# 64 unused bytes per partition between the weight buffers and the buffers of split tokens

## The chip, the cores and the metric

The kernel runs on one core of a Trainium2 chip. The metric is the device time of one execution in microseconds; the time before is the median of three runs. One more execution was taken with the hardware profiler, and all rows below come from it.

## What is computed

The reference is attention with a sigmoid in place of the softmax, for 8 batches of 12 heads with 448 tokens and 64 features a head, followed by a layer that takes the maximum of three products and multiplies it by an output matrix:

```python
scores = q @ k.T / sqrt(64) - log(448)
x = (1 / (1 + exp(-scores))) @ v          # then heads side by side: 3584 x 768
h = maximum(maximum(x @ w1, x @ w2), x @ w3)
out = h @ w_out                           # all four matrices 768 x 768
```

Everything is float32.

## The kernel before

**Two stages.** Attention runs first, 24 steps of four heads each; the results go to DRAM. Behind it runs the maxout stage: four matrices (w1, w2, w3 and the output matrix), each multiplied with the tokens of eight batches. The stage is tiled in visits: 4 groups of output columns (`STAGES`) times 4 pairs of batches, 16 visits; in each visit three products `q`, and each of these by a scheme of Strassen's kind, with seven block products (`PRODUCTS`) instead of eight. The operands of the block products are sums and differences of blocks: `a11`, `s2`, ... for weights, `b11`, `t2`, ... for tokens.

**Split operands.** Each operand is kept as two float32r tiles, a rounded `hi` and the remainder `lo`; a block product is the sum of lo x hi, hi x lo and hi x hi over three blocks of 128 features, which makes 9 matmuls of 128 x 128 weights by 448 token columns. So the stage has 16 x 3 x 7 x 9 = 3024 matmuls, all issued by one line, 476, in `product`. Weights are the stationary operand, tokens the moving one. Two of the 3024 are made 30 columns wider (`wide`, 478 columns): the first matmul of block product 1 in visit 0, and the first of block product 4 in visit 11, second product. The 30 extra columns are read from the next block of the same tile, and their results are used by nobody.

**What is where in SBUF.** Pools take their place in the order in which they are opened. These stay for the whole kernel: `w` (42 tiles of split weights, 7 operands x 3 products x hi and lo, 1536 bytes per partition each), `ws` (weights before the split, 1536 bytes each), `xs` (tokens before the split, 5376 bytes each), `m` (4 result tiles of 1792 bytes), and `xo` (hi and lo of the first two token operands, 5376 bytes each). Behind `xo` come attention's pools, which are closed at its end: `qk`, `hl`, `dec`, `sq`, `v`, `a`. Their place is taken by the maxout stage's further pools: `xs2`, `xo2` (hi and lo of the other five token operands), `c` and `dec2`. A matmul of line 476 reads 128 columns of weights at `k * P` (512 bytes times k) and a block of tokens at `xt[:, k]` (1792 bytes times k).

**Order.** Every instruction is pinned to program order on its engine, so the order of work is the order of the text. All loads and stores but half of the last one are issued by SyncE; VectorE computes the `lo` tiles (lines 121, 231, 294), ScalarE the sigmoid (282), the `hi` tiles (227) and copies out of PSUM (583), GpSimd the sums of blocks (108, 196).

In attention, line 312 computes the scores as three float32r products, in pairs of two matmuls with 64 rows of weights each; lines 336 and 347 weigh the values in plain float32. All operands of these lines come from pools that are opened behind `xo`.

Of the kernel before, what the change touches and what calls it, by code (L numbers as in the profile page):

```python
# [8 lines left out]
F32 = mybir.dt.float32  # L9
# [8 lines left out]
P = 128  # L18
D = 64

LEAST = 1.125 * 2.0**-15

PRODUCTS = (
    ("a11", "b11", 0),
# [10 lines left out]
def attention_then_maxout(  # L35
# [30 lines left out]
    def pool(stack, name, bufs, **kw):  # L66
        return stack.enter_context(tc.tile_pool(name=name, bufs=bufs, **kw))
# [2 lines left out]
    ws_p = pool(ctx, "ws", 1)  # L70
    xs_p = [pool(ctx, "xs", 1)]
    m_p = pool(ctx, "m", 1)
    xo_p = [pool(ctx, "xo", 1)]
    ps_av = pool(ctx, "ps_av", 1, space=PSUM)

# [47 lines left out]
    def decoding(dec_p, todo, bufs, ahead, square_p):  # L123
# [11 lines left out]
        def decode(raw, out):  # L135
# [17 lines left out]
            pin(nc.vector.scalar_tensor_tensor(  # L153
                out=out, in0=square, scalar=LEAST**2, in1=bits.bitcast(F32),
                op0=ALU.is_ge, op1=ALU.mult,
# [504 lines left out]
```

## Time and profile before

| | |
|---|---|
| median of three runs | 864.51 us (864.01 to 864.61) |
| profiled execution, span from first to last instruction | 861.9 us |
| TensorE matmul busy | 857.6 us, 99% |
| VectorE, ScalarE, GpSimd busy | 619.9, 413.3, 173.5 us |
| maxout stage (line 476) in the chain that ended last | 613.13 us of it |

The profiled span leaves out what lies before the first and behind the last instruction; it stands 2.6 us under the median. "PE" is TensorE's matmuls and "PEld" its weight loads, which run beside them; a matmul's own duration in the trace is longer than the distance to the next one, since matmuls are pipelined, so pace is read from the starts. The names of tiles are cut at their first digit or so: `xhi_t` stands for all `hi` tiles of the token operands t1 to t4, `whi_s` for the weights s1 to s4. `a<-b` is written from b.

### The profile page before, as it was taken

The page shows a single profiled execution, that of the slowest core. Times are in us where ns is not written, and L with a number is a line of the kernel's source. Part 1 is how long each engine was busy: PE and PEld are TensorE (multiplying, and loading weights), DVE is VectorE, ACT ScalarE, POOL GpSimd, SP SyncE. Part 2 cuts the span into 40 slices and gives each one's busy share as a digit, 9 for nine tenths or more (in the row PEclk, how much of TensorE's full clock was granted, in tenths as well). Part 3 has the DMA queues.
Part 4 walks back from the last instruction along what each step waited for, and adds up shares of the span by engine and source line. Part 5 has one row for each costly group of instructions (what it writes and reads, how often), then busy time and mean ns, then how long its engine had stood idle before and what let it go on. Part 6 is the DMA issues. An engine that isn't in the chain of part 4 may idle for free.

```text
span 861.9 us, 14260 instructions
## 1 busy us (share of the span) xinstructions
PE 857.6 (99%) x5446; PEld 706.5 (82%) x5446; DVE 619.9 (72%) x885; ACT 413.3 (48%) x545; POOL 173.5 (20%) x148
## 2 busy tenths in 40 slices
PE   9999999999999999999999999999999999999998
PEld 5555555555579999999999999999999999999997
DVE  5677668877795775787887698778778887736542
ACT  6888888888862340423434252234325252423310
POOL 0010020202115337121000021200002544560600
PEclk9999999999999999999999999999999999999999
DMA  8657776786684537326563823465472516153412
GB/s 293 209 209 242 246 253 231 257 295 220 214 288 175 184 147 250 125 75 205 207 248 113 324 80 97 161 254 198 161 290 99 186 43 238 69 202 123 154 65 86
DMA packets 74628, 161.96 MB, mean 188 GB/s; under 512 B 6976, under 2 KB 54080, under 8 KB 74560
## 3 DMA queue, kind: packets, MB, share of 16 engines
q1 hardware_dynamic: 74416, 160.94, 53.0%
q8 instruction: 43, 0.70, 0.3%
q14 instruction: 25, 0.20, 0.1%
q10 hardware_dynamic: 144, 0.11, 0.0%
HBM read 109.90 MB, written 51.12 MB: 187 GB/s over the span
## 4 chain that ended last, share of the span: by engine, by line
PE 99%; DVE 0%; DVEq 0%; issue 0%
PE ps_y L476 71%; PE ps_s L312 9%; PE ps_s L336 7%; PE ps_av L336 6%; PE ps_s L347 2%; PE ps_s L325 2%; PE ps_av L312 2%; PE ps_s L383 0%; PE ps_av L325 0%; PE ps_av L347 0%; DVE m L548 0%; DVEq L656 0%
## 5 line engine op out<-in xcount | busy, mean ns | idle before, releaser
L476 PE MATMUL ps_y<-xhi_t,whi_s 128*128 128x448 f32 x432 | 157.9, 365 | 0.0
L476 PE MATMUL ps_y<-xhi_t,wlo_s 128*128 128x448 f32 (+1 forms) x432 | 157.8, 365 | 0.0
L476 PE MATMUL ps_y<-xlo_t,whi_s 128*128 128x448 f32 x432 | 157.8, 365 | 0.0
L282 ACT ACTIVATE a<-ps_s,bias_s 128x896 f32<-128x896 f32 x121 | 114.5, 1016 | 10.2 <-PE ps_s L312 10.2
L476 PE MATMUL ps_y<-xhi_b,wlo_a 128*128 128x448 f32 x288 | 105.3, 366 | 0.0
L476 PE MATMUL ps_y<-xlo_b,whi_a 128*128 128x448 f32 x288 | 105.2, 365 | 0.0
L476 PE MATMUL ps_y<-xhi_b,whi_a 128*128 128x448 f32 x288 | 105.2, 365 | 0.0
L583 ACT COPY p<-ps_y 128x448 f32<-128x448 f32 x48 | 25.5, 531 | 157.6 <-PE ps_y L476 157.6
L108 POOL TENSOR_TENSOR ws_s<-ws_a,ws_a 128x384 f32<-128x384 f32 x12 | 14.2, 1180 | 417.9 <-DMA ws_a<-w_dram 312.8
L476 PEld LDWEIGHTS ps_y<-xhi_t,whi_s 128*128 128x128 f32 x432 | 81.2, 188 | 6.4
L476 PEld LDWEIGHTS ps_y<-xlo_t,whi_s 128*128 128x128 f32 x432 | 81.2, 188 | 6.4
L476 PEld LDWEIGHTS ps_y<-xhi_t,wlo_s 128*128 128x128 f32 x432 | 81.2, 188 | 6.3
L557 DVE TENSOR_TENSOR m<-ps_y,u 128x448 f32<-128x448 f32 x71 | 43.9, 621 | 53.3 <-PE ps_y L476 53.3
L544 ACT COPY m<-ps_y 128x448 f32<-128x448 f32 x24 | 12.8, 533 | 124.8 <-PE ps_y L476 112.6
L586 DVE TENSOR_TENSOR u<-ps_y,p 128x448 f32<-128x448 f32 x48 | 29.9, 623 | 53.9 <-PE ps_y L476 50.3
L196 POOL TENSOR_TENSOR xs_t<-xs_b,xs_t 128x448 f32<-128x448 f32 x48 | 59.8, 1272 | 38.9 <-PE ps_s L325 26.8
L231 DVE TENSOR_TENSOR xlo_t<-xs_t,xhi_t 128x1344 fp32r<-128x1344 f32 x42 | 66.7, 1589 | 0.0
L231 DVE TENSOR_TENSOR xlo_b<-xs_b,xhi_b 128x1344 fp32r<-128x1344 f32 x42 | 66.5, 1584 | 0.0
L142 ACT ACTIVATE c<-wraw 128x384 f32<-128x384 f32 x48 | 27.4, 570 | 75.5 <-DVE m L563 44.0
L336 PE MATMUL ps_av<-a,v 64*64 64x448 f32 x576 | 62.6, 536 | 0.0
L227 ACT CAST xhi_t<-xs_t 128x1344 fp32r<-128x1344 f32 x41 | 54.2, 1323 | 12.4 <-PE ps_y L476 8.8
L336 PE MATMUL ps_s<-a,v 64*64 64x448 f32 x576 | 59.7, 545 | 0.0
(89 smaller groups left out, 1769.0 us busy)
## 6 DMA issues: line engine op xcount, KB each, us to landing
qk<-qk SPq DMA_DIRECT2D x47, 448.0 KB, 4.6
xs_b<-x_dram SPq DMA_DIRECT2D x30, 672.0 KB, 6.9
wraw<-w SPq DMA_DIRECT2D x36, 384.0 KB, 4.8
xs_t<-t_dram SPq DMA_DIRECT2D x18, 672.0 KB, 8.0
v<-v SPq DMA_DIRECT2D x24, 448.0 KB, 5.5
h_dram<-m SPq DMA_DIRECT2D x48, 224.0 KB, 1.9
xs_b<-h_dram SPq DMA_DIRECT2D x16, 672.0 KB, 6.2
x_dram<-m SPq DMA_DIRECT2D x47, 224.0 KB, 3.0
```

The lines of the kernel that those rows point to most:

```text
L142: pin(nc.scalar.activation(out=square, in_=high.bitcast(F32), func=AF.Square))
L196: pin(nc.gpsimd.tensor_tensor(out=r[name][:, k], in0=r[in0][:, k], in1=r[in1][:, k], op=ALU.subtract))
L227: pin(copy(out=hi, in_=r[name]))
L231: pin(nc.vector.tensor_tensor(out=lo, in0=x, in1=hi.bitcast(F32), op=ALU.subtract))
L282: pin(nc.scalar.activation(out=a, in_=banks[:, :, :S], func=AF.Sigmoid, bias=bias_s, scale=scale))
L312: pin(nc.tensor.matmul(bank[e][:, :S], kt[r, S + c * P : S + (c + 1) * P], qt[r, :S], start=n == 0, stop=n == len(terms) - 1,))
L325: pin(nc.tensor.matmul(ps[g * D : (g + 1) * D, e, :S], t[r, S + C * P :], t[r, :S], start=True, stop=True,))
L336: pin(nc.tensor.matmul(ps[e * D : (e + 1) * D, :S], vt[rows, (g * C + c) * 2 + e], chunks[c][rows, e], start=c == 0 and not (ahead and r = ...
L476: pin(nc.tensor.matmul(ps[:, :cols], wt[:, k * P : (k + 1) * P], moving, start=first and n == 0, stop=n == len(terms) - 1, skip_group_chec ...
L557: pin(nc.vector.tensor_tensor(out=m[name], in0=y, in1=add, op=ALU.add))
L583: pin(nc.scalar.copy(out=p1, in_=ps[0][:, :S]))
L586: pin(nc.vector.tensor_tensor(out=u2, in0=ps[1][:, :S], in1=p1, op=ALU.add))
```

## The change

A pool with one tile of 16 float32 per partition is opened between `m` and `xo`. No instruction reads or writes the tile.

```diff
 LEAST = 1.125 * 2.0**-15
+
+
+SHIFT = 16
 
@@
     xs_p = [pool(ctx, "xs", 1)]
     m_p = pool(ctx, "m", 1)
+
+    pool(ctx, "shift", 1).tile([P, SHIFT], F32, name="shift")
     xo_p = [pool(ctx, "xo", 1)]
     ps_av = pool(ctx, "ps_av", 1, space=PSUM)
```

## Rows read from the trace of the kernel before

**Rows 1.** The page's busy times, then stretches of the maxout stage (busy us, count)
```profile
PE 857.6 (99%) x5446; PEld 706.5 (82%) x5446; DVE 619.9 (72%) x885; ACT 413.3 (48%) x545; POOL 173.5 (20%) x148
core 0: us, PE busy (x) PEld busy (x) DVE busy (x) ACT busy (x) POOL busy (x), PEclk, DMA share, GB/s
250.00:350.00 100.00, 100.00 (x495) 92.76 (x494) 66.87 (x82) 26.46 (x30) 49.85 (x40) 1.00 0.55 201
450.00:550.00 100.00, 100.00 (x495) 92.75 (x495) 82.40 (x123) 36.60 (x54) 9.53 (x8) 1.00 0.43 153
690.00:790.00 100.00, 100.00 (x495) 92.74 (x494) 69.69 (x81) 40.15 (x49) 44.74 (x35) 1.00 0.36 128
```

**Rows 2.** The chain that ended last, in order of time: start us, us, what
```profile
18.39 1.21 PE ps_s L312 x12
...
28.45 1.24 PE ps_s L312 x12
...
245.25 613.13 PE ps_y L476 x3024
858.38 0.02 issue
858.40 0.39 DVE m L548
858.80 0.30 DVEq L656
```

**Rows 3.** TensorE's instructions in order of time, entry into the maxout stage
```profile
start us, us, engine line op out<-in xcount [idle before <-releaser]
...
245.49 0.36 PE L476 MATMUL ps_y<-xlo_b,whi_a 128*128 128x448 f32 x1
245.69 0.37 PE L476 MATMUL ps_y<-xhi_b,whi_a 128*128 128x448 f32 x1
245.90 0.37 PE L476 MATMUL ps_y<-xhi_b,wlo_a 128*128 128x448 f32 x1
...
247.14 0.38 PE L476 MATMUL ps_y<-xhi_t,wlo_s 128*128 128x478 f32 x1
247.36 0.36 PE L476 MATMUL ps_y<-xlo_t,whi_s 128*128 128x448 f32 x1
247.55 0.36 PE L476 MATMUL ps_y<-xhi_t,whi_s 128*128 128x448 f32 x1
```

**Rows 4.** The same, in the middle of the stage (with weight loads) and its end
```profile
400.16 0.36 PE L476 MATMUL ps_y<-xhi_b,whi_a 128*128 128x448 f32 x1
400.36 0.37 PE L476 MATMUL ps_y<-xhi_t,wlo_s 128*128 128x448 f32 x1
400.37 0.19 PEld L476 LDWEIGHTS ps_y<-xlo_t,whi_s 128*128 128x128 f32 x1
400.57 0.36 PE L476 MATMUL ps_y<-xlo_t,whi_s 128*128 128x448 f32 x1
400.77 0.36 PE L476 MATMUL ps_y<-xhi_t,whi_s 128*128 128x448 f32 x1
400.97 0.37 PE L476 MATMUL ps_y<-xhi_t,wlo_s 128*128 128x448 f32 x1
...
858.00 0.37 PE L476 MATMUL ps_y<-xhi_b,whi_s 128*128 128x448 f32 x1
```

**Rows 5.** Groups of instructions of line 476: busy us, mean ns | idle before
```profile
L476 PE MATMUL ps_y<-xhi_t,whi_s 128*128 128x448 f32 x432 | 157.9, 365 | 0.0
L476 PE MATMUL ps_y<-xhi_b,whi_a 128*128 128x448 f32 x288 | 105.2, 365 | 0.0
L476 PE MATMUL ps_y<-xhi_b,wlo_a 128*128 128x448 f32 x287 | 105.0, 366 | 0.0
L476 PEld LDWEIGHTS ps_y<-xhi_t,whi_s 128*128 128x128 f32 x432 | 81.2, 188 | 6.4
```

**Rows 6.** Waits: engine, line, waited for: us in total, times, longest
```profile
ACT p L583 <- PE ps_y L476: 157.6, 41, 12.2
DVE m L557 <- PE ps_y L476: 53.3, 41, 3.0
PE ps_s L383 <- PEq L650: 0.8, 1, 0.8
```

**Rows 7.** The page's DMA issues: count, KB each, median us to landing
```profile
qk<-qk SPq DMA_DIRECT2D x47, 448.0 KB, 4.6
xs_t<-t_dram SPq DMA_DIRECT2D x18, 672.0 KB, 8.0
```

## The prediction

> **What bounds the kernel now.** I read four views in this order: the page's busy times, the chain of work that ended last, TensorE's instructions in order of time, and the waits. The page has TensorE busy for 857.6 of 861.9 us [rows 1]; the next engine, VectorE, has 72%. The chain says the same in order: from 245.25 us on it is one piece of 613.13 us, the 3024 matmuls of line 476, followed by 0.39 us of VectorE and 0.30 us for the issue of a DMA [rows 2]. The list of waits has a single entry for TensorE's matmuls, 0.8 us before the first one [rows 6]; everything else waits for TensorE (ScalarE 157.6 us at line 583, VectorE 53.3 us at line 557). So only one thing can move the end: the distance from one matmul's start to the next. The granted clock reads 1.00 in every stretch of the maxout stage that I looked at [rows 1], so it is 2.4 GHz throughout and not part of the question.
>
> **What a step costs today.** The maxout stage starts with matmuls at 245.69, 245.90, ... 247.14 us [rows 3]: seven steps in 1.45 us, 207 ns each. At 247.14 stands the one matmul with 478 columns (`wide`); the steps behind it are shorter. From 247.55 us [rows 3] to the last start at 858.00 us [rows 4] lie 3012 steps (12 of the 3024 matmuls are over, the last has no step behind it), so 610.45 us / 3012 = 202.7 ns. The same two paces stand in attention: a burst of scores of 12 matmuls, issued in pairs, takes 1.24 us at 28.45 us and 1.21 us at 18.39 us [rows 2], that is 206.7 and 201.7 ns a pair. So one and the same stream of instructions has two paces, some 4.0 ns apart, and which of them it takes is settled where the stream is entered or kicked, not by what it computes. Neither pace is the 448 columns alone: 448 columns at 2.4 GHz are 186.7 ns. Some 16 ns of every step are lost, 16.0 x 3012 = 48 us in all. While a matmul streams its columns the next weights are loaded: the load starts within 0.01 us of the matmul and lasts 188 ns [rows 4, 5]. So both operands are read side by side for nearly the whole step, and the change moves one of them against the other.
>
> **What the change does to the operands.** The tile is written and read by nobody; no instruction, wait, DMA or order of issue is added or removed. What it can do is to move the pools behind it by 64 bytes per partition: the split tokens (`xo`), and, since attention's pools and those of the maxout stage are opened later, all of these. The weights (`w`), their stage (`ws`), the first token pool (`xs`) and `m` stay. All tiles of these pools hold a multiple of 256 bytes per partition (1536 = 6 x 256 for weights, 5376 = 21 x 256 for tokens, 1792 = 7 x 256 for `m`), and the slices that a matmul reads start at multiples of 512 (weights) or 1792 bytes (tokens). So today the distance between the start of any moving operand and of any stationary operand of line 476 is a multiple of 256 bytes; afterwards it is a multiple of 256 plus 64, for all 3024 of them. In attention both operands lie behind the new tile, so their distance stays what it was, and only their place against a boundary of 128 or 256 bytes moves.
>
> What does the trace say of such distances? The stage pairs 42 weight tiles with 14 token tiles in all sorts of multiples of 256, and the groups of line 476 have means of 365 or 366 ns whichever tiles they read [rows 5]; the 100 us stretches hold 495 matmuls each time [rows 1]. So the multiple does not matter. The remainder of 64 stands nowhere in this trace. Its price must be bounded from both sides: a step can hardly be shorter than the weight load of 188 ns [rows 5], so 202.7 - 188 = 14.7 ns x 3012 = 44 us is the most that can be gained (820); and the slowest pace that the trace knows, 206.7 to 207 ns, costs 4.0 x 3012 = 12.1 us. What the DMAs, VectorE and ScalarE do on the moved tiles (tokens and `qk` land in 4.6 to 8.0 us [rows 7]) I cost at nothing: TensorE's matmuls wait for them nowhere but for 0.8 us at the start [rows 6]. If that cover went, it would show as a wait of TensorE, and 0.8 us is the most that can be gained there.
>
> Between 188 and 207 I take 200 ns, and this is a choice. Starts are given to 0.01 us; steps read 0.19 (once, 247.36 to 247.55 [rows 3]), 0.20 and 0.21 [rows 4], and the mean of 202.7 says that the readings of 0.21 are not rare. If two reads that lie 64 bytes further apart meet less often, a stream that keeps to the middle reading is the row nearest to today's pace. 2.7 ns x 3012 = 8.1 us less: 861.9 - 8.1 = 853.8 for the profiled execution. The median of the runs, 864.51, lies 2.6 us above the profiled span; with the same 2.6 us the forecast is 856.4.
>
> A rule speaks against this. The Trainium skill, "SBUF — State Buffer", section "A bandwidth-pool intuition that's wrong (but worth ruling out)", gives TensorE a second, independent read port for LDWEIGHTS; by that the weight load would not disturb the columns, and the time would stay 864.5. The trace does not bear it out fully, since the lost 16 ns stand there, but it does not show that the two reads are the reason either. The Trainium skill, "TensorE: Matmul & The Clock Gate", section "Back-to-back issue gap", gives N / 2.4 + 2.5 ns a step, 189.2 ns here; the sum by that would be 13.5 x 3012 = 41 us less (824), an estimate from that page, while the trace's step is 202.7.
>
> **The rivals.** (a) No change: the 16 ns have nothing to do with where operands lie, or only with remainders that 64 bytes do not touch, or the allocator gives a tile without a user no place and the program is the same. For it: the multiples of 256 show no influence at all, and the two paces stand side by side at one and the same placement. Against it: that one stream has two paces says that the loss is a matter of how two periodic things meet, and a shift of one read against the other is of that sort. Time: 864.5, within 0.8 us.
>
> (b) Slower: the stage keeps the 206.7 ns pace. It enters the stage in it today and leaves it at one place only, the matmul of 478 columns at 247.14 us [rows 3], whose 30 extra columns fit today's placement. If at the new distance this kick leads back into the slow pace, nothing else in the stage kicks before the second wide matmul in visit 11 (some 72% through the stage). Price 4.0 x 3012 = 12.1 us, 876.6; if the second kick rescues the rest, 4.0 x 2168 = 8.7 us, 873.2 (2168 steps lie between the two). It decides at the first step behind 247.14: 0.207 or less than 0.203.
>
> (c) Much faster: the loss is all two reads meeting, and 64 bytes take it away; then steps come down towards the weight load's 188 ns, 820 to 840. For it speaks only that 16 ns are there to be had; against it, that the trace shows no step anywhere near it.
>
> **How the numbers follow.** Faster, by the forecast's mechanism: 0.37; its own range is 846 (a step of 196.6 ns, about two of the distances between the two paces below the fast one, (202.7 - 196.6) x 3012 = 18.4 us) to 862.7. Much faster (c): 0.08. No change (a): 0.33, of which 0.05 for a tile that gets no place. Slower (b): 0.22. A difference of 0.2%, 1.7 us, is about what a measurement of this kernel can tell from no change. So faster 0.45, same 0.33, slower 0.22. The range reaches from 846 over the unchanged 864.5 to 877, the slow pace kept to the end; outside it are (c) and no more than 0.05 of the others.
>
> **What would show it.** In the profile after, the piece of line 476 in the chain must be shorter than 613.13 us, by 8 us if I am right, with the number of instructions the same, attention still ending near 245.2 us (its operands move together), and the steps in the middle of the stage reading 0.20 without a 0.21 among five. Rival (a) shows the same 613.1 us and the same steps. Rival (b) shows 0.207 at 250 us and 621 to 625 us. The prediction is also wrong if the gain stands in attention, where I expect none, or if TensorE gets waits, which none of the cases has.

## The result

The changed kernel takes 856.59 us (median of four runs, 855.95 to 857.06) against 864.26 us for the kernel before (four runs, 863.37 to 864.61): a ratio of 0.9912, 95% interval 0.9898 to 0.9926, 0.9% faster. The forecast was 856.4.

Its profiled execution spans 854.1 us, 7.8 less than before. The page's busy times, and one stretch of 100 us of the maxout stage:

```profile
PE 849.8 (99%) x5446; PEld 704.9 (83%) x5446; DVE 617.7 (72%) x885; ACT 412.8 (48%) x545; POOL 175.0 (20%) x148
...
690.00:790.00 100.00, 100.00 (x501) 93.74 (x500) 67.36 (x79) 39.83 (x50) 42.25 (x32) 1.00 0.42 144
```

The counts of instructions are those of [rows 1]; TensorE is busy 7.8 us less, and 501 matmuls fit into the 100 us that held 495. The chain of the changed kernel has the difference in one piece:

```profile
245.45 605.13 PE ps_y L481 x3024
850.59 0.02 issue
850.61 0.39 DVE m L553
851.00 0.30 DVEq L661
```

Line 481 is line 476 of before, moved by five lines. Its 3024 matmuls take 605.13 instead of 613.13 us [rows 2]. Attention ends at 245.45 instead of 245.25 us, and the three pieces at the end are the same. TensorE's instructions at the entry, in the middle and at the end, which answer to [rows 3, 4]:

```profile
245.70 0.36 PE L481 MATMUL ps_y<-xlo_b,whi_a 128*128 128x448 f32 x1
245.90 0.36 PE L481 MATMUL ps_y<-xhi_b,whi_a 128*128 128x448 f32 x1
246.10 0.36 PE L481 MATMUL ps_y<-xhi_b,wlo_a 128*128 128x448 f32 x1
...
247.10 0.36 PE L481 MATMUL ps_y<-xhi_b,whi_a 128*128 128x448 f32 x1
247.30 0.38 PE L481 MATMUL ps_y<-xhi_t,wlo_s 128*128 128x478 f32 x1
247.51 0.36 PE L481 MATMUL ps_y<-xlo_t,whi_s 128*128 128x448 f32 x1
247.71 0.36 PE L481 MATMUL ps_y<-xhi_t,whi_s 128*128 128x448 f32 x1
...
400.11 0.36 PE L481 MATMUL ps_y<-xhi_t,whi_s 128*128 128x448 f32 x1
400.31 0.36 PE L481 MATMUL ps_y<-xhi_t,wlo_s 128*128 128x448 f32 x1
400.51 0.36 PE L481 MATMUL ps_y<-xlo_t,whi_s 128*128 128x448 f32 x1
...
850.20 0.37 PE L481 MATMUL ps_y<-xhi_b,whi_s 128*128 128x448 f32 x1
```

Two things are to be seen. The stage no longer begins at 207 ns a step: from 245.70 to 247.10 us there are seven steps in 1.40 us, 200 ns each, ahead of any kick. And from 247.71 to 850.20 us, 3012 steps, it is 602.49 us / 3012 = 200.0 ns, against 202.7.

### The profile page after: what moved, and what is told of

Read it like the earlier page. It is cut to its first block, busy times and chain, and to the rows that moved or that the text cites. A ratio compares the mean times of both kernels' runs of the same rounds, so it can differ in the third digit from the quotient of the medians.

```text
span 854.1 us, 14260 instructions
## 1 busy us (share of the span) xinstructions
PE 849.8 (99%) x5446; PEld 704.9 (83%) x5446; DVE 617.7 (72%) x885; ACT 412.8 (48%) x545; POOL 175.0 (20%) x148
## 4 chain that ended last, share of the span: by engine, by line
PE 99%; DVE 0%; DVEq 0%; issue 0%
PE ps_y L481 71%; PE ps_s L317 9%; PE ps_s L341 7%; PE ps_av L341 6%; PE ps_s L352 2%; PE ps_s L330 2%; PE ps_av L317 2%; PE ps_s L388 0%; PE ps_av L330 0%; PE ps_av L352 0%; DVE m L553 0%; DVEq L661 0%
## 5 line engine op out<-in xcount | busy, mean ns | idle before, releaser
L481 PE MATMUL ps_y<-xhi_t,whi_s 128*128 128x448 f32 x432 | 155.9, 361 | 0.0
```

Source lines behind the costliest of these rows:

```text
L481: pin(nc.tensor.matmul(ps[:, :cols], wt[:, k * P : (k + 1) * P], moving, start=first and n == 0, stop=n == len(terms) - 1, skip_group_chec ...
```

## Experiments: what sets the pace

Theory D says that the distance between the starts of the moving operand (tokens) and the stationary one (weights), modulo 256 bytes, sets the pace. Rival P says that the place of the tokens against a boundary does. Rival E says that the pace is settled once, at the entry.

**Both operands moved.** The 64 bytes ahead of the weights instead of behind them:

```diff
+    pool(ctx, "shift", 1).tile([P, SHIFT], F32, name="shift")
     w_p = pool(ctx, "w", 1)
...
-    pool(ctx, "shift", 1).tile([P, SHIFT], F32, name="shift")
```

> The 64 bytes stand ahead of the weight pool, so weights and tokens both move by 64 bytes and their distance is again a multiple of 256, as before; the tokens lie where the changed kernel has them. Theory D (the distance between the start of the moving and of the stationary operand sets the pace): steps of 202.7 ns, 613 us for the 3024 matmuls, 864.3 us in all. Rival P (where the tokens start against a boundary of 128 or 256 bytes sets it): 200.0 ns, 605 us, 856.6 us.

Measured: 864.19 us (median of ten runs), a ratio to before of 0.9998 (0.9989 to 1.0008). The stage in the chain:

```profile
245.00 613.14 PE ps_y L481 x3024
```

The tokens lie where the changed kernel has them, and nothing is gained. P is out; so is any gain from where DMAs or the other engines find the tokens.

**Other sizes of the unused tile**, `SHIFT = 8`, `32` and `64` in place of 16:

> 32 bytes instead of 64. Theory D: a distance never seen so far, so a pace of its own is possible between 188 and 207 ns; if only whole units of 64 bytes count, 202.7 ns and 864.3 us. Rival P: the tokens are off their boundary again, 202.7 ns and 864.3 us.

> 128 bytes instead of 64. Theory D: if distances repeat after 128 bytes, 202.7 ns and 864.3 us; if after 256, a pace of its own, or 200.0 ns and 856.6 us. Rival P with a boundary of 128 or 256 bytes: the tokens start 64 bytes past it, 202.7 ns and 864.3 us.

> 256 bytes instead of 64, so the distance is a multiple of 256 as before, with the tile still there. Theory D and rival P both: 202.7 ns, 613 us for the stage, 864.3 us. If the time is 856.6 us, what helped was the tile itself or anything else that came with it, and not the remainder of 64.

Measured: 869.66, 867.47 and 863.89 us, one run each, against 864.15 for before. The stage in the chain, for 32, 128 and 256 bytes in this order:

```profile
245.84 618.48 PE ps_y L481 x3024
```

```profile
245.00 617.13 PE ps_y L481 x3024
```

```profile
245.42 613.13 PE ps_y L481 x3024
```

256 bytes give the stage of before to 0.01 us: it is the remainder that counts, not that a tile stands there. 32 and 128 bytes give paces of their own (starts in the trace: 204.4 and 204.0 ns), and both are slower than before. So the distance matters, and most of its values do not help.

**A distance for each product.** Unused tiles between the weights of the three products of a visit give each product its own distance:

```diff
     def w_tiles(q, name):
+        if q in w_pad:
+            w_p.tile([P, w_pad.pop(q)], F32, name=f"wpad{q}")
         hi = w_p.tile([P, HP], F32R, name=f"whi_{name}_{q}")
```

> The same with 0 bytes for product 0, 192 for product 1 and 64 for product 2. Theory D: 200.0 ns in product 2, as in the changed kernel, and 202.7 ns in product 0 as in the kernel before, or 206.7 where the slow pace is entered anew, alternating in every visit; product 1 unknown, between 200 and 207 ns. If product 1 had 202.7 ns: 864.3 - 2.7 ns x 1008 = 861.6 us. Rival E: one pace throughout.

Measured: 860.83 us (one run, as are all that follow but one). The stage takes 610.03 us in the chain. TensorE's instructions in visit 8: the 10th and the 63rd matmul of product 0 (distance 0), of product 1 (192) and of product 2 (64), with 53 steps between them:

```profile
552.26 0.36 PE L485 MATMUL ps_y<-xhi_t,wlo_s 128*128 128x448 f32 x1
...
563.00 0.36 PE L485 MATMUL ps_y<-xhi_b,whi_s 128*128 128x448 f32 x1
...
565.02 0.37 PE L485 MATMUL ps_y<-xhi_t,wlo_s 128*128 128x448 f32 x1
...
575.74 0.37 PE L485 MATMUL ps_y<-xhi_b,whi_s 128*128 128x448 f32 x1
...
577.75 0.36 PE L485 MATMUL ps_y<-xhi_t,wlo_s 128*128 128x448 f32 x1
...
588.35 0.36 PE L485 MATMUL ps_y<-xhi_b,whi_s 128*128 128x448 f32 x1
```

10.74, 10.72 and 10.60 us over 53 steps are 202.6, 202.3 and 200.0 ns, in one and the same visit, and the paces come back in every visit. That is D, and it rules E out: within a visit the stream changes its pace from product to product, as the distance changes. The sum fits: 1008 matmuls at 2.7 ns and 1008 at 0.4 ns less than 202.7 are 3.1 us, and 613.13 - 610.03 = 3.1.

The same with 224, 160 and 96 bytes:

> Pads between the weights of the three products of a visit give each product its own distance: 224 bytes (mod 256) for product 0, 160 for product 1, 96 for product 2; each has 63 matmuls in a row, 1008 in all. Theory D (distance sets the pace): three paces that change every 63 matmuls, each the same in all 16 visits; 32 bytes gave 204.4 and 128 gave 204.0 ns, so between 200 and 207 ns, 856 to 876 us. Rival E (the pace is settled once, where the stage is entered, by whatever the placement does there): one pace from the first kick to the end.

Measured: 872.12 us, stage 621.06 us. Products 0 and 2 hold 204.4 and 205.3 ns in all visits, as expected. Product 1, at 160 bytes, does not: the 10th and 63rd matmul of it in visit 0 and in visit 1 are

```profile
260.44 0.36 PE L485 MATMUL ps_y<-xhi_t,wlo_s 128*128 128x448 f32 x1
...
271.04 0.37 PE L485 MATMUL ps_y<-xhi_b,whi_s 128*128 128x448 f32 x1
...
298.91 0.37 PE L485 MATMUL ps_y<-xhi_t,wlo_s 128*128 128x448 f32 x1
...
309.87 0.36 PE L485 MATMUL ps_y<-xhi_b,whi_s 128*128 128x448 f32 x1
```

10.60 and 10.96 us: 200.0 ns in the first visit and 206.7 ns from the second on. So D needs a supplement: the distance sets which paces there are, and at 160 bytes there are two. Distance 0 has two as well, 206.7 at the entry [rows 3] and 202.7 behind it. Which of the two is taken at distance 0 depends on what ran ahead, as the kernel without its wider matmuls shows below; that it is so at 160 bytes too is a guess.

**Finer distances**, with the weights of a product in one tile and an offset inside (`hi = w_all[q][:, at : at + HP]`):

> Distances that are no multiples of 32: 48 bytes for product 0, 80 for product 1, 56 for product 2 (the weights of each product in one tile, with an offset inside). Known so far: 0 gives 202.7 ns, 32 gives 204.4, 64 gives 200.0, 96 gives 205.3. If the pace follows a unit of 32 bytes or more, 48 and 56 give 204.4 and 80 gives 200.0; if a finer unit counts, paces of their own between 188 and 207 ns, and a better one than 200.0 may stand among them.

> Three more distances: 16 bytes for product 0, 240 for product 1, 72 for product 2. Known: 48 gives 204.4, 56 and 64 give 200.0, 80 gives 203.3, 0 gives 202.7, 224 gives 204.4 ns. Theory D, with a pace for each distance that was the same in all visits so far: three steady paces between 200 and 207 ns; 72 bytes should tell whether 200.0 is a narrow place (over 202 ns) or one that reaches from 56 to 72 (200.0 ns). Against the theory: a pace that changes between visits at one distance.

Measured: 864.47 and 869.67 us. The 10th and the 63rd matmul of product 2 in visit 8, at 56 bytes and at 72 bytes:

```profile
580.04 0.36 PE L491 MATMUL ps_y<-xhi_t,wall 128*128 128x448 f32 x1
...
590.64 0.57 PE L491 MATMUL ps_y<-xhi_b,wall 128*128 128x448 f32 x2
```

```profile
582.25 0.37 PE L491 MATMUL ps_y<-xhi_t,wall 128*128 128x448 f32 x1
...
593.09 0.36 PE L491 MATMUL ps_y<-xhi_b,wall 128*128 128x448 f32 x1
```

10.60 and 10.84 us over 53 steps are 200.0 and, in this visit, 204.5 ns. All paces that the runs gave, each over 53 steps of a product from the starts in the trace, or over the whole stage:

| distance, bytes | 0 | 16 | 32 | 48 | 56 | 64 | 72 | 80 | 96 | 128 | 160 | 192 | 224 | 240 |
|---|---|---|---|---|---|---|---|---|---|---|---|---|---|---|
| ns a step | 202.7, 206.7 | 203.3 | 204.4 | 204.4 | 200.0 | 200.0 | 204.4 | 203.3 | 205.3 | 204.0 | 200.0, 206.7 | 202.2 | 204.4 | 206.7 |

The place with 200.0 ns is narrow: 48 and 72 bytes are both at 204.4. None of the 14 distances has a pace under 200.0.

The paces are means, and the single steps behind them repeat in a short pattern. The trace keeps starts to the nanosecond. In the middle of the stage, and to within a nanosecond, the steps go 202, 203, 202, 199, 207 ns and again at 0 bytes (the run with both operands moved), 202, 201, 197 at 64 bytes (the changed kernel), and 200 each time at 56 bytes. The means between 200.0 and 206.7 stand close to simple fractions of the way: 202.2 at a third, 202.7 at two fifths, 203.3 at a half, 204.0 at three fifths, 204.4 at two thirds, 205.3 at four fifths. Something periodic is at work, then; what it is, no run shows.

## Experiments: the kick, attention, and the cause

**Without the two wider matmuls**, `wide = ()`, in the kernel before and in the changed one:

> The kernel before without the two matmuls that are 30 columns wider. If the pace of 206.7 ns at the entry is a state that stays until something kicks it: 206.7 ns for the whole stage, 12.1 us more, 876.4 us. If it is a transient that ends by itself within some dozen steps: 864.2 us.

> The changed kernel without the two wider matmuls. It entered the stage at 200 ns without a kick. If at a distance of 64 there is only that pace: 200.0 ns throughout, 856.6 us. If the wide matmuls are what keeps it there: a slower pace, up to 206.7 ns and 876.8 us.

Measured: 876.35 and 855.96 us (864.75 for before beside them). The stage in the chain, first of before without the kick, then of the changed kernel without it:

```profile
245.84 625.16 PE ps_y L476 x3024
```

```profile
245.16 605.46 PE ps_y L481 x3024
```

625.16 us are 206.7 ns for 3024 steps: at distance 0 the slow pace of the entry lasts to the end of the stage, and with the wider matmuls it ends at the first of them [rows 3]. At distance 64 no kick is needed.

**The same distance in attention.** The key half of the split tiles 192 bytes further on, so that the score matmuls too have their operands 64 bytes (modulo 256) apart:

```diff
-            hi = hl_p.tile([P, 2 * S], F32R, name="hi")
+            hi = hl_p.tile([P, 2 * KEY + 32], F32R, name="hi")     # KEY = S + 48
...
-                        bank[e][:, :S], kt[r, S + c * P : S + (c + 1) * P], qt[r, :S],
+                        bank[e][:, :S], kt[r, at : at + P], qt[r, :S],
```

> The changed kernel, and in attention the key half of the split tiles starts 192 bytes further, so that in the score matmuls, too, the moving operand starts a multiple of 256 plus 64 bytes from the stationary one. Theory D: the pairs of score matmuls go from 202.7 to 200.0 ns (the one burst at 206.6 perhaps too); some 430 pairs x 2.7 ns = 1.2 us, 855.4 us. Rival P (place, not distance) and the rival that pairs of 64 rows are bound otherwise: 202.7 ns a pair, 856.6 us.

Measured: 856.46 us (four runs, 856.15 to 857.05), ratio to before 0.991 (0.9893 to 0.9926): no better than the changed kernel. Yet the pace did change. Two score matmuls of the same burst, first of the changed kernel, then of this one:

```profile
107.15 0.36 PE L317 MATMUL ps_s<-hi,lo 64*128 64x448 f32 x2
...
109.58 0.36 PE L317 MATMUL ps_s<-hi,lo 64*128 64x448 f32 x2
```

```profile
107.12 0.36 PE L333 MATMUL ps_s<-hi,lo 64*128 64x448 f32 x2
...
109.52 0.37 PE L333 MATMUL ps_s<-hi,lo 64*128 64x448 f32 x2
```

Twelve pairs take 2.43 us in one and 2.40 us in the other, 202.5 and 200 ns. What became of the gain stands in the waits of the weight loads, in the 22 full steps of attention from 16 to 236 us, the changed kernel first:

```profile
PEld ps_s L341 <- ACT a L287: 6.6, 22, 0.3
```

```profile
PEld ps_s L357 <- ACT a L287: 7.2, 22, 0.3
```

Behind the scores the first weighing waits for the sigmoid of line 287, and it now waits 0.6 us longer. Summed over the starts of these 22 steps, the score matmuls are 0.54 us shorter and the gap from the last of them to the first weighing 0.63 us longer. So here ScalarE's sigmoids set when the weighing can begin, and a faster burst of scores only waits for them. The forecast of 855.4 for this kernel left that out.

**Half the weights.** On the placement of before, eight of nine matmuls load 64 columns of weights, so the kernel leaves out part of the product:

```diff
-                ps[:, :cols], wt[:, k * P : (k + 1) * P], moving,
+                ps[:wide_w, :cols], wt[:, k * P : k * P + wide_w], moving,     # wide_w = P if n == 0 else P // 2
```

> The placement before (distance 0), but eight of the nine matmuls of each block product load 64 columns of weights instead of 128, and so leave out half of the output features in eight of nine terms; the 448 moving columns, the number of instructions and their order stay. Theory W (the 16 ns a step over 186.7 are lost where the reads of the weight load meet those of the moving columns): half the weights read, so about half the loss in those eight steps, 194 to 196 ns; the stage shortens by 3024 x 8/9 x 7 ns = 19 us to about 845 us. Rival M (the loss belongs to the stream of moving columns or to the change from one matmul to the next): 202.7 ns stays, 864.2 us.

Measured: 865.36 us against 864.38 for before. A weight load of this kernel, and its stage in the chain:

```profile
L477 PEld LDWEIGHTS ps_y<-xhi_t,whi_s 128*64 128x64 f32 x432 | 58.0, 134 | 30.1
...
246.03 613.99 PE ps_y L477 x3024
```

The loads last 134 instead of 188 ns, and the steps are 203.0 ns, not 195. Theory W falls as it was priced: the lost time does not follow how much is read for the weights. It fits M, a loss that belongs to the moving columns or to the change from one matmul to the next; which of the two was not told apart. A loss of a fixed size where each weight load meets the columns is not excluded: the loads are shorter here, but as many, and they start where they did. And M by itself does not say why the place of the weights should matter, which the run with both operands moved shows.

## Why the prediction was right, and where its reasons were not

**The bound** held in the maxout stage. TensorE's steps were the only thing that moved the end: 8.0 us in the stage, 7.8 us in the span, 7.7 us between the medians. For attention it was put too widely: of TensorE's waits [rows 6] lists those of the matmuls alone, and the weight loads of the kernel before wait there for ScalarE, 7.2 us in all; it is this wait that grew and took the gain in the run with attention's operands moved:

```profile
PEld ps_s L336 <- ACT a L282: 7.2, 24, 0.3
```

**The size** was right: 200 ns chosen, 200.0 measured; 605.0 us forecast for the stage (613.13 - 8.1), 605.13 found. But it came out by luck. It was a choice between 188 and 207 ns on the readings of 0.19, 0.20 and 0.21 us, and the runs show how little those readings held: a tile of 32, 128, 160, 192, 224 or 240 bytes would have had the same argument, and five of these six have a pace over 202.7 ns, 160 with a second one of 200.0. Of the 13 distances other than 0 that were run, only 56 and 64 give 200.0 throughout. The prediction had the stream keep to one middle reading, but its steps are 202, 201 and 197 ns in turn. One figure of the range was misread: 196.6 ns lies 6.1 ns under today's pace, one and a half times the 4.0 ns between the two paces and not about two.

**The reason** was right in one half. The distance between the operands is what counts: both moved together give 864.19 us, and the pace changes from product to product with the distance. The other half, that the time is lost where the reads of weights and columns meet, is not shown: with half the weights read a step still takes 203.0 ns, so the loss does not grow with what is read, and where it arises stays open. Nor did the trace say which way 64 bytes would work; the chance of 0.22 for slower was too low for a shift of unknown effect, since ten of the 13 distances are slower than 202.7 ns, 160 bytes in one of its two paces.

**The rivals.** (a), no change, is excluded by the result; its part on an unplaced tile by the pace as well. (b), the slow pace kept, had the right price: 876.6 us was worked out, and 876.35 is what the kernel before takes without its kick. Its condition did not come up, since at 64 bytes the stage is entered at 200 ns and stays there without the kick. (c) is excluded for this distance; 200.0 is the fastest pace found anywhere.

**What was to be seen** was seen: the shorter piece in the chain, the same instructions, steps of 0.20 without a 0.21 at 400 us, and attention without a gain. One item was wrong: TensorE gets no waits, it said. In the changed kernel one step is longer, and its weight load waits for VectorE:

```profile
507.61 0.61 DVE L567 TENSOR_TENSOR c<-ps_y,u 128x448 f32<-128x448 f32 x1
...
508.27 0.19 PEld L481 LDWEIGHTS ps_y<-xhi_b,wlo_s 128*128 128x128 f32 x1 [0.17 <-DVE c L567]
508.31 0.44 PE L481 MATMUL ps_y<-xhi_b,wlo_s 128*128 128x448 f32 x1
...
508.58 0.36 PE L481 MATMUL ps_y<-xlo_b,whi_s 128*128 128x448 f32 x1
```

The step takes 0.27 us instead of 0.20. The load waits until VectorE's addition of line 567 has read its bank `ps_y`, at 508.22 us; in the kernel before the same addition ended 0.80 us ahead of the load (510.62 and 511.43 us). Past the stage's first load, such waits for VectorE, for an addition or for a `lo` tile, are listed only in the runs whose whole stage has a distance of 64 bytes: one here, four without the kick, one with attention's operands moved. At a slower pace none is listed, so at 200 ns a step VectorE is close to being a second bound.

**The rules.** The Trainium skill, "SBUF — State Buffer", section "A bandwidth-pool intuition that's wrong (but worth ruling out)", gives the weight loads a read port of their own. The run with half the weights agrees with it, as the amount of weights read changes a step by 0.3 ns only; but where the weights stand against the columns changes it by up to 6.7 ns, so by the measurement the two are not independent in every respect. The Trainium skill, "TensorE: Matmul & The Clock Gate", section "Back-to-back issue gap", gives the formula behind the 189.2 ns for an isolated matmul, and says that in a stream of weight loads and matmuls both set the spacing; the prediction took it for the step of such a stream. 189.2 ns appear in no run; the nearest is 200.0.

## What to carry to other kernels

Where TensorE is busy without a gap, the distance between matmul starts is the quantity to read, over some dozens of steps and not from the duration of one; if it is longer than the columns need and differs between stretches that do the same work, placement or the way in may be behind it. Then try distances between the two operands in small steps and measure each, since neither sign nor size can be read off the trace. And look at who sets the end before spending a faster TensorE elsewhere: in attention here, shorter steps bought nothing.

## What was not expected of the hardware

A stream of float32r matmuls of 448 columns, each with its own weight load, at the full granted clock, takes between 200.0 and 206.7 ns a step depending on the distance of its operands modulo 256 bytes, with two paces at 0 bytes (202.7 and 206.7) and at 160 bytes (200.0 and 206.7). At 0 bytes the slow pace lasts for a whole stage of 625 us, and one matmul of 30 more columns ends it. Loading 64 instead of 128 columns of weights, 134 instead of 188 ns, leaves the step at 203.0 ns. Why the distance counts, and why the pattern repeats after 256 bytes (0 and 256 agree to 0.01 us over the stage), stays open.
